# A written-out schedule replaced: two row tiles and both filter pieces at the head of the loads, and a new order of all steps

## Chip, cores and metric

The kernel runs on one core of a Trainium2 chip. The metric is the device time of one execution in microseconds; lower is better. The time before is 196.86 us, the median of three runs (196.56 to 197.38).

## What is computed

Sequence length 2048, width 512, feed-forward width 1792, one batch, bf16.

```python
xn = layernorm(A_q)                       # over the last axis
# s: a short causal convolution, a gate, a long causal convolution
k_shift[t] = sum_j k[t-3+j] * shift_k[:, j]          # 4 taps
kv = k_shift * v
y  = causal_conv(kv, ssm_k) + kv * ssm_D             # 2048 taps for each of 512 channels, by FFT in the reference
s  = xn * y
# g: a gated feed-forward block
g  = silu( (gelu(xn @ w_gate) * (xn @ w_up)) @ w_down )
out = A_q + s * g
```

## The kernel before

The feed-forward half works on four quarters of the sequence, q = 0 to 3, each of four row tiles of 128 rows. For each quarter and each of 14 column groups m of w_gate and w_up (Wg, Wu), TensorE makes two products of four matmuls (steps psg and psu), ScalarE takes gelu of the first (GE), and VectorE multiplies it with the second (HT). Four matmul groups with w_down (Wd) for each row tile follow (psd). The first two column groups of quarter 0 are done in halves of 256 columns, so that they can begin when only row tiles 0 and 1 are there. Their input xnT is the normalised x (XN), transposed by TensorE (psxn) and copied out of PSUM by ScalarE or VectorE.

The long convolution is a two-stage Fourier transform done with matmuls. The filter arrives as four pieces of 512 KB, Hn0 to Hn3. Hn0 and Hn1 are transposed by TensorE (psh), copied out (HTr), and multiplied with the transform table F (steps ps1H, copies AH); the result is written to DRAM (ZH, eight writes of 256 KB issued on ScalarE's queue). Hn2 and Hn3 are permuted by four ScalarE copies into HP, transposed by DMA into HTD, and go through ps1J, copies AJ and eight more writes to ZH on SP's queue. AJ has four buffers, so the fifth copy needs the first write to have landed. The signal kv is made by VectorE from KK, V and four tap rows SKB (copied by GpSimd from SKR): 32 long instructions, each quarter ending in KV0 to KV3. It goes through ps1K and AK to ZK. Second stages (psf for the filter, psk for the signal, psi for the way back) use 32-row matmuls; BH, BK, HS, HW, BO and ZI are their buffers, MI and G1 their tables, which three DMA transpositions on SP's queue make. The last matmuls (psy) bring y back into sequence order, and VectorE joins both halves. Weights come in four pieces, of 2, 4, 4 and 4 column groups.

Nothing on the chip decides an order. The program makes 788 tasks with numbers; the string `SEQ` lists these numbers, and every engine's instructions are emitted in the order of that list. A trailing `b` gives a task to the second engine that it allows (VectorE instead of ScalarE). Loads and most writes are issued on SP's queue in the order of the list too, so each queue runs in order and a step that waits holds up all behind it on its engine. The string `ORDER` numbers the loads: `x01` is row tile 0 of x alone, `x22` tiles 2 and 3, `h` a filter piece, `w` a pair of w_gate and w_up pieces, `s` the taps, `d` half of w_down. The class `Sched` computes planned times for the tasks in the list's order; on the chip this matters only in one way: when a step takes a buffer or PSUM bank from a pool, it is given the one that is planned to be free first.

```python
t.start, t.eng = max(base, free.get(eng, 800.0)), eng
...
f, b.slot = b.pool.find()
```

Eleven matmuls on zeros (`warm_up`) precede the first real step.

Of the kernel before, what the change touches and what calls it, by code (L numbers as in the profile page):

```python
# [16 lines left out]
NT = 16  # L17
# [5 lines left out]
LAST = [(0, 384), (384, 512)]  # L23
TURN = 8192
N_WARM = 11
ORDER = "x01 h0 x11 h1 x22 w0 w1 h2 h3 D0 w2 s0 k0 v0 x1 w3 k1 v1 d0 d1 k2 v2 k3 v3 x2 x3"
SEQ = (
# [22 lines left out]
)  # L50
NF_BANKS = 4
ISSUE = 470.0
LOAD_NS = {("x0_", 262144): 1400.0, ("x0_", 131072): 450.0, 262144: 900.0, 524288: 1350.0, ("x", 524288): 2100.0, ("h", 524288): 1300.0, ("wg", 524288): 1550.0, ("wu", 524288): 1450.0, 917504: 2620.0, ("sk", 524288): 1500.0, 344064: 1250.0, 46080: 350.0, 3072: 100.0, 1024: 200.0}
W_XT, W_SW, W_BK, W_BH, W_ZI, W_BI, W_ZK, W_MI, W_G1 = 1665000, 600000, 555000, 703000, 333000, 640000, 490000, 740000, 222000
NC_PAIRS = 4
SMALL = 1.15 * 262144
# [235 lines left out]
class Sched:  # L292
# [2 lines left out]
    SEM = 90.0  # L295
    DMA_LAT = 2000.0
    LOAD_LAT = 2450.0
    HEDGE = 600.0
    DMA_BW = 370.0
    SHARE_BW = 300.0  # L300
    FIRST = {"loads": 1050.0, "SP": 30500.0}
    DRAIN = 121.0
    EARLY, TAKEN, SHARED, WAIT = (0.0, 1.0), 1400.0, 46000.0, 3300.0
    LANDS = (3150.0, 3490.0, 5770.0)

    def __init__(self):
        self.tasks = []
# [35 lines left out]
                t.deps.append(d)  # L343

    def run(self):
        free = dict(self.FIRST)
        pipe = 0.0
        n_loads = 0
        order = []
        pmode = 0  # L350
        for name in SEQ.split():
            t = self.tasks[int(name.rstrip("b"))]
            eng, dur = t.opts[name[-1] == "b"]
            base = 0.0
            for d in t.deps:
                base = max(base, d.end if eng == d.eng == "PE" else d.end + d.lat + (self.SEM if not d.nbytes or eng != "PE" else 400.0 if d.eng == "loads" else self.HEDGE))
            for b in t.w:
                if b.pool is not None and b.slot is None:
                    f, b.slot = b.pool.find()
                    b.pool.take(b.slot)  # L360
                    base = max(base, f + self.SEM)
            t.start, t.eng = max(base, free.get(eng, 800.0)), eng
            free[eng] = t.end = t.start + dur + (self.DRAIN if eng == "PE" and t.mode != pmode else 0.0)
            pmode = t.mode if eng == "PE" else pmode
            if eng == "loads":
                free[eng] = t.start + dur * (self.EARLY[1] if t.start < self.EARLY[0] else 1.0)
                if n_loads < len(self.LANDS):
                    free[eng] = self.LANDS[n_loads] - self.LOAD_LAT
                n_loads += 1
                t.end = free[eng] + self.LOAD_LAT  # L370
            elif t.nbytes:
                en = t.end
                if en < self.SHARED:
                    free["loads"] += self.TAKEN
                pipe = max(pipe, en + self.DMA_LAT / 2) + t.nbytes / (self.SHARE_BW if en < self.SHARED else self.DMA_BW)
                t.end = pipe + self.DMA_LAT / 2 + (self.WAIT if en < self.SHARED else 0.0)
            for b in set(t.r + t.w):
                b.left -= 1
                b.last_end = max(b.last_end, t.end + t.lat)
                if b.left == 0 and b.pool is not None:  # L380
                    b.pool.release(b.slot, b.last_end)
            order.append(t)
        assert sorted(t.n for t in order) == list(range(len(self.tasks)))
        return order
# [6 lines left out]
def act(n, sb=False):  # L391
    return 170.0 + n * 0.833 + (30.0 if sb else 0.0)


def dve(n, rate):
    return 150.0 + n / 0.96 / rate


def build_kernel(nc, A_q, A_k, A_v, A_shift_k, A_ssm_k, A_ssm_D, B_w_gate, B_w_up, B_w_down, out):
    with ExitStack() as es0:  # L400
# [56 lines left out]
        Hn = at("Hn", [128, KD, S_LEN], BF16, g_at)  # L457
        HTr = at("HTr", [128, NT // 2, DM], BF16, kk_at - 16384)
        HP = at("HP", [128, NT, 2, 128], BF16, kk_at - 8192)
# [139 lines left out]
        def op(engs, fn, r=(), w=(), rr=(), ww=(), lat=0.0, after=()):  # L599

            def emit(e):
                R = rr() if callable(rr) else rr
                W = ww() if callable(ww) else ww
                trk.op(e, lambda h: fn(e, h), r=R, w=W)
            return S.add(engs, emit, r=r, w=w, lat=lat, after=after)
# [284 lines left out]
        h_perm, h_dtr = [], []  # L890
        d_htd = [dsem(f"d_htd{hf}") for hf in range(2)]
        for hf in range(2):
            for k in range(2):
                h_perm.append(op([("ACT", act(1024, True)), ("DVE", dve(1024, 1))], lambda e, h, hf=hf, k=k: copy(e, h, HP[:, 8 * hf:8 * hf + 8, k, :], Hn[:, 2 + k, :].rearrange("p (a t) -> p t a", t=NT)[:, 8 * hf:8 * hf + 8, :]),
                                 r=[bHn[2 + k]], w=[bHP[hf]], rr=[R_Hn[2 + k]], ww=[R_HP[hf]]))
        for hf in range(2):
            def dtr(e, hf=hf):
# [294 lines left out]
        for j in range(8):  # L1192
            p = B(f"psy{j}", pC)
# [93 lines left out]
```

## Time and profile before

| | |
|---|---|
| median of three runs | 196.86 us |
| profiled execution | 195.77 us |
| its span, first to last instruction | 194.0 us |
| TensorE busy | 187.5 us (97%) |
| VectorE busy | 159.8 us (82%) |
| ScalarE busy | 125.5 us (65%) |
| DMA | 49.19 MB, mean 254 GB/s |
| granted TensorE clock | 1.000 |

A row of the timeline gives the start in us, the time from the first start to the last end of the merged instructions, the engine, the line, the operation, output and input tiles, the shape and the count; in brackets stands the idle time of the engine ahead of it and what ended it. `SPq` and `ACTq` rows are DMA issues on a queue. A matmul row's length contains the modelled end of the last matmul, so the distance between starts is the better measure of pace. Line 618 is the helper through which all plain matmuls go, line 609 the helper for ScalarE's copies, line 590 the helper for DMAs.

### The profile page before, as it was taken

The numbers are of one execution on the slowest core, as the hardware profiler recorded it, in microseconds if no ns is written. First come the engines' busy times: TensorE is split into PE (matmuls) and PEld (weight loads), VectorE is DVE, ScalarE is ACT, GpSimd is POOL, SyncE is SP. The second block draws the span as 40 slices with busy tenths as digits, with TensorE's granted clock in tenths as the row PEclk, the third lists the DMA queues.
The fourth block names the chain that finished last, engine by engine and source line by source line (L and its number), as shares of the span: only waits on it lengthen the run. The fifth ranks groups of instructions, "written<-read, shape, count | busy, mean of one in ns | idle before, by whom it ended". The sixth has DMA issues, their size and how long they took to land.

```text
span 194.0 us, 3492 instructions
## 1 busy us (share of the span) xinstructions
PE 187.5 (97%) x1364; PEld 85.0 (44%) x1377; DVE 159.8 (82%) x245; ACT 125.5 (65%) x170; POOL 14.0 (7%) x32
## 2 busy tenths in 40 slices
PE   7799999999998999999999999999999999999993
PEld 2594544444443444443434433433444434444442
DVE  7599699998999993977788789878897963588993
ACT  6787999979876978868648767756577531222121
POOL 6412420000000000020300000000000000000000
PEclk9999999999999999999999999999999999999999
DMA  5999999999999859999999991893714344939333
GB/s 165 327 322 349 377 403 315 188 217 375 368 363 355 242 210 231 384 345 283 277 306 221 318 312 41 291 332 106 237 37 184 105 150 135 402 109 363 126 139 135
DMA packets 46102, 49.19 MB, mean 254 GB/s; under 512 B 12803, under 2 KB 39943, under 8 KB 46086
## 3 DMA queue, kind: packets, MB, share of 16 engines
q1 hardware_dynamic: 37510, 42.67, 69.8%
q10 hardware_dynamic: 8576, 6.29, 10.1%
q8 instruction: 11, 0.18, 0.4%
q14 instruction: 5, 0.04, 0.1%
HBM read 27.39 MB, written 14.68 MB: 217 GB/s over the span
## 4 chain that ended last, share of the span: by engine, by line
PE 87%; DMA 7%; ACT 2%; issue 1%; SPq 1%; DVE 1%
PE psall L618 80%; PE psall L1028 5%; DMA Hn<-in_A_ssm_k_dram 3%; DMA ZH<-X 3%; SPq L590 1%; PE psall L854 1%; ACT G L609 1%; PE psall L878 1%; ACT X L609 1%; ACT ASX L609 0%; ACT GE L1137 0%; DVE G L1175 0%; DVE G L1174 0%; ACT G L1172 0%
## 5 line engine op out<-in xcount | busy, mean ns | idle before, releaser
L618 PE MATMUL psall<-xnT,Wu 128*128 128x512 bf16 (+1 forms) x232 | 55.8, 372 | 0.0
L618 PE MATMUL psall<-xnT,Wg 128*128 128x512 bf16 (+1 forms) x232 | 55.3, 372 | 0.0
L618 PE MATMUL psall<-Wd,HT 128*128 128x512 bf16 (+2 forms) x231 | 50.8, 366 | 0.7 <-issue 0.5
L1140 DVE TENSOR_TENSOR HT<-psall,GE 128x512 bf16<-128x512 f32 x54 | 36.7, 685 | 15.2 <-PE psall L618 13.6
L1137 ACT ACTIVATE GE<-psall 128x512 bf16<-128x512 f32 x54 | 31.7, 601 | 12.6 <-PE psall L618 12.2
L618 PEld LDWEIGHTS psall<-Wd,HT 128*128 128x128 bf16 x238 | 22.4, 98 | 25.9 <-issue 1.1
L618 PEld LDWEIGHTS psall<-xnT,Wu 128*128 128x128 bf16 x232 | 21.6, 98 | 25.9 <-issue 3.8
L618 PEld LDWEIGHTS psall<-xnT,Wg 128*128 128x128 bf16 x232 | 21.9, 98 | 25.3 <-issue 1.3
L609 ACT ACTIVATE X<-psall 128x1024 bf16<-128x1024 f32 (+1 forms) x18 | 15.1, 846 | 3.8 <-DMA ZH<-X 3.3
L609 ACT ACTIVATE HS<-psall 128x1024 bf16<-128x1024 f32 x14 | 13.7, 1022 | 4.2 <-PE psall L1028 4.2
L1164 ACT ACTIVATE G<-psall 128x512 bf16<-128x512 f32 x12 | 7.0, 597 | 12.8 <-PE psall L618 12.4
L1011 DVE TENSOR_TENSOR KAC<-KAC,KTM 128x2048 bf16<-128x2048 bf16 x12 | 14.6, 1218 | 0.1
L1009 DVE TENSOR_TENSOR KTM<-KK,SKB 128x2048 bf16<-128x2048 bf16 x12 | 14.6, 1217 | 0.0
L609 ACT ACTIVATE BO<-psall 128x1024 bf16<-128x1024 f32 x9 | 9.1, 1023 | 8.2 <-PE psall L1028 7.7
L821 DVE BATCH_NORM_STATS2 stats<-X 128x6 f32<-128x512 bf16 x16 | 10.3, 677 | 3.9 <-DMA X<-in_A_q_dram 3.9
L609 ACT ACTIVATE KB<-psall 128x1024 bf16<-128x1024 f32 x11 | 11.0, 1021 | 3.6 <-PE psall L1028 3.6
L609 ACT ACTIVATE AST<-psall 128x1024 bf16<-128x1024 f32 x12 | 12.3, 1031 | 1.2 <-PE psall L618 1.0
L612 DVE CAST BO<-psall 128x1024 bf16<-128x1024 f32 x7 | 8.5, 1223 | 3.7 <-PE psall L1028 3.7
L1172 ACT ACTIVATE G<-psall 128x512 bf16<-128x512 f32 (+2 forms) x5 | 2.6, 512 | 13.1 <-PE psall L618 13.1
L1091 DVE TENSOR_TENSOR HW<-KB,HW 128x1024 bf16<-128x1024 bf16 x16 | 10.9, 682 | 0.0
L1091 DVE TENSOR_TENSOR HS<-KB,HS 128x1024 bf16<-128x1024 bf16 x16 | 10.8, 682 | 0.0
L618 PE MATMUL psall<-V,F 128*128 128x512 bf16 x30 | 8.8, 379 | 0.4 <-ACT ASX L609 0.3
(83 smaller groups left out, 172.2 us busy)
## 6 DMA issues: line engine op xcount, KB each, us to landing
BH<-ZH SPq DMA_DIRECT2D x8, 512.0 KB, 6.3
HW<-HS SPq DMA_DIRECT2D x16, 256.0 KB, 2.9
BK<-ZK SPq DMA_DIRECT2D x8, 512.0 KB, 5.1
ZI<-BO ACTq DMA_DIRECT2D x16, 256.0 KB, 2.9
BI<-ZI SPq DMA_DIRECT2D x8, 512.0 KB, 4.1
ZK<-AST SPq DMA_DIRECT2D x6, 512.0 KB, 3.7
Hn<-in_A_ssm_k_dram SPq DMA_DIRECT2D x4, 512.0 KB, 8.4
KK<-in_A_k_dram SPq DMA_DIRECT2D x4, 512.0 KB, 8.8
```

The costliest lines, as they stand in the source:

```text
L609: return h.activation(o, i, ACTF.Copy, scale=scale)
L612: return h.tensor_copy(o, i)
L618: return h.matmul(o, lhsT=l, rhs=r, start=st, stop=sp)
L821: t_stats[t] = op([("DVE", 670.0)], lambda e, h, t=t: h.bn_stats(stats[:, t, :], X[:, t, :]), r=[bX[q][t % 4]], w=[bst[t]], rr=[R_X[t]], w ...
L1009: op([("DVE", dur)], lambda e, h, j=j, m=m: h.tensor_tensor(KTM[:, m.slot, :, :], kk(j), sk(j), ALU.mult), r=need + [bSKB[j], a], w=[m], r ...
L1011: op([("DVE", dur)], lambda e, h, m=m: h.tensor_tensor(KAC[:, a.slot, :, :], KAC[:, a.slot, :, :], KTM[:, m.slot, :, :], ALU.add), r=[m], ...
L1028: trk.op("PE", lambda h: h.matmul(ps(s, i)[b, :], lhsT=wt(col)[a, :], rhs=data(col)[a, :], start=n < 16, stop=n >= len(todo) - 16, tile_po ...
L1091: return hd.tensor_tensor(o, flat(KB, kb[h]), o, ALU.mult)
L1137: op([("ACT", act(512))], lambda e, h: h.activation(GE[:, g.slot, :], bank(pg), ACTF.Gelu_apprx_tanh), r=[pg], w=[g], rr=lambda: R_bank(pg ...
L1140: op([("DVE", dve(512, 1))], lambda e, h: h.tensor_tensor(HT[:, q % 2, m, :], bank(pu), GE[:, g.slot, :], ALU.mult), r=[pu, g], w=[bHT[q][m]],
L1164: op([("ACT", act(n))], lambda e, h, g=g, pc=pc: h.activation(g, pc(), ACTF.Tanh, scale=0.5), r=[p], w=[bt], rr=lambda p=p: R_bank(p), ww= ...
L1172: op([("ACT", act(n))], lambda e, h, g=g, pc=pc: h.activation(g, pc(), ACTF.Silu), r=[p], w=[bt], rr=lambda p=p: R_bank(p), ww=rg, after=z ...
```

## The change

`ORDER` starts with `x02 h0 h1 x22` instead of `x01 h0 x11 h1 x22`: row tiles 0 and 1 come as one load of 256 KB, and the first two filter pieces precede tiles 2 and 3. There are 787 tasks instead of 788, all numbers from 20 on are lower by one, and the whole of `SEQ` is new. The planner's constants and its model of transfers are replaced: eight noted landing times for the first loads instead of three, an allowance of 900 ns behind a later load, and the transfers of loads and writes in one line. The four HP copies are now allowed on ScalarE alone, at 2090 ns.

In names, the first loads on SP's queue are, before: X0, X1, Hn0, X2+X3, Hn1, Wg0, Wu0, X of quarter 1, Wg1, KK0, D, Wu1, Hn2, KK0, Wg2, SKR, KK0, KK1, Wu2, Wg3, Wu3, Hn3, V3, V0, KK2, HTD0, HTD1. After: X0+X1, Hn0, Hn1, X2+X3, Wg0, Wu0, X of quarter 1, Wg1, KK0, Wu1, D, Hn2, KK0, SKR, Wg2, KK0, KK1, Wu2, Hn3, Wg3, KK4, V0, KK2, Wu3, V3, HTD1, KK3, HTD0.

The first steps of TensorE before: psh0 (two), psxn0_0, psxn0_1, three ps1H halves, psh1 (two), psg0_0 first half. After: psh0 (two), psh1, ps1H5, psh1, ps1H4, ps1H6, ps1H2, psxn0_0, psxn0_1, three ps1H halves, psu0_0 first half, psxn0_2, psxn0_3. The first four writes to ZH stand in ScalarE's list between its first gelus; before, one did.

```diff
-ORDER = "x01 h0 x11 h1 x22 w0 w1 h2 h3 D0 w2 s0 k0 v0 x1 w3 k1 v1 d0 d1 k2 v2 k3 v3 x2 x3"
+ORDER = "x02 h0 h1 x22 w0 w1 h2 h3 D0 w2 s0 k0 v0 x1 w3 k1 v1 d0 d1 k2 v2 k3 v3 x2 x3"
 SEQ = (
-    "17 19 18 0 3 1 2 4 8 5 7 11 21 6 9 51 12 66 67 68 74 20 69 76 75 50 10 77 13 53 22 83 23 84 87 118 70 108 71 72 113 55 73 88 78 79 54 370 52 "
...
+    "0 2 1 3 11 5 4 8 9 12 10 13 7 6 17 18 19 20 50 49 65 53 66 73 67 68 75 74 52b 76 55b 69 51 107 108 54 102 112 96 70 71 77 82 56 72 83 104 "
...
-LOAD_NS = {("x0_", 262144): 1400.0, ("x0_", 131072): 450.0, 262144: 900.0, 524288: 1350.0, ("x", 524288): 2100.0, ...
+LOAD_NS = {("x0_", 262144): 1200.0, ("x0_", 131072): 450.0, 262144: 900.0, 524288: 1430.0, ("x", 524288): 1500.0, ...
-    HEDGE = 600.0
-    DMA_BW = 370.0
-    SHARE_BW = 300.0
-    FIRST = {"loads": 1050.0, "SP": 30500.0}
+    HEDGE, LATE = 1500.0, 900.0
+    DMA_BW = 350.0
+    AHEAD, ISSUE = 6000.0, (480.0, 3000.0)
     DRAIN = 121.0
-    EARLY, TAKEN, SHARED, WAIT = (0.0, 1.0), 1400.0, 46000.0, 3300.0
-    LANDS = (3150.0, 3490.0, 5770.0)
+    LANDS = (4100.0, 5590.0, 6950.0, 8300.0, 9200.0, 10100.0, 11500.0, 12950.0)
...
+            t.eng = eng
             if eng == "loads":
...
+                t.start = max(base, free["SP"])
+                dma = max(dma, t.start + self.LOAD_LAT) + dur
                 if n_loads < len(self.LANDS):
-                    free[eng] = self.LANDS[n_loads] - self.LOAD_LAT
+                    dma = self.LANDS[n_loads]
...
+                if t.nbytes:
+                    t.end = dma = max(dma, t.end + self.DMA_LAT) + t.nbytes / self.DMA_BW
...
-                h_perm.append(op([("ACT", act(1024, True)), ("DVE", dve(1024, 1))], ...
+                h_perm.append(op([("ACT", 2090.0)], ...
```

More of the change, by code (lines that the diff above doesn't have):

```diff
@@ L52 @@
 ISSUE = 470.0
-LOAD_NS = {("x0_", 262144): 1400.0, ("x0_", 131072): 450.0, 262144: 900.0, 524288: 1350.0, ("x", 524288): 2100.0, ("h", 524288): 1300.0, ("wg", 524288): 1550.0, ("wu", 524288): 1450.0, 917504: 2620.0, ("sk", 524288): 1500.0, 344064: 1250.0, 46080: 350.0, 3072: 100.0, 1024: 200.0}
+LOAD_NS = {("x0_", 262144): 1200.0, ("x0_", 131072): 450.0, 262144: 900.0, 524288: 1430.0, ("x", 524288): 1500.0, ("h", 524288): 1400.0, ("wg", 524288): 1700.0, ("wu", 524288): 1550.0, 917504: 2900.0, ("sk", 524288): 1500.0, 344064: 1300.0, 46080: 350.0, 3072: 100.0, 1024: 200.0}
 W_XT, W_SW, W_BK, W_BH, W_ZI, W_BI, W_ZK, W_MI, W_G1 = 1665000, 600000, 555000, 703000, 333000, 640000, 490000, 740000, 222000
@@ L345, in run @@
     def run(self):
-        free = dict(self.FIRST)
-        pipe = 0.0
+        free = {"SP": 700.0}
+        dma = 0.0
         n_loads = 0
@@ L355, in run @@
             for d in t.deps:
-                base = max(base, d.end if eng == d.eng == "PE" else d.end + d.lat + (self.SEM if not d.nbytes or eng != "PE" else 400.0 if d.eng == "loads" else self.HEDGE))
+                base = max(base, d.end if eng == d.eng == "PE" else d.end + d.lat + (self.SEM if not d.nbytes or eng in ("SP", "loads") or d.end < 11000.0 else self.LATE if d.eng == "loads" or eng != "PE" else self.HEDGE))
             for b in t.w:
@@ L361, in run @@
                     base = max(base, f + self.SEM)
-            t.start, t.eng = max(base, free.get(eng, 800.0)), eng
-            free[eng] = t.end = t.start + dur + (self.DRAIN if eng == "PE" and t.mode != pmode else 0.0)
-            pmode = t.mode if eng == "PE" else pmode
+            t.eng = eng
             if eng == "loads":
-                free[eng] = t.start + dur * (self.EARLY[1] if t.start < self.EARLY[0] else 1.0)
+                t.start = max(base, free["SP"])
+                dma = max(dma, t.start + self.LOAD_LAT) + dur
                 if n_loads < len(self.LANDS):
-                    free[eng] = self.LANDS[n_loads] - self.LOAD_LAT
+                    dma = self.LANDS[n_loads]
                 n_loads += 1
[L370 to L376, printed above, removed]
+                t.start = max(t.start, dma - dur - self.LOAD_LAT - self.AHEAD)
+                free["SP"] = t.start + (self.ISSUE[1] if dur > 3000.0 else self.ISSUE[0])
+                t.end = dma
+            else:
+                t.start = max(base, free.get(eng, 800.0))
+                free[eng] = t.end = t.start + dur + (self.DRAIN if eng == "PE" and t.mode != pmode else 0.0)
+                pmode = t.mode if eng == "PE" else pmode
+                if t.nbytes:
+                    t.end = dma = max(dma, t.end + self.DMA_LAT) + t.nbytes / self.DMA_BW
             for b in set(t.r + t.w):
@@ L893, in build_kernel @@
             for k in range(2):
-                h_perm.append(op([("ACT", act(1024, True)), ("DVE", dve(1024, 1))], lambda e, h, hf=hf, k=k: copy(e, h, HP[:, 8 * hf:8 * hf + 8, k, :], Hn[:, 2 + k, :].rearrange("p (a t) -> p t a", t=NT)[:, 8 * hf:8 * hf + 8, :]),
+                h_perm.append(op([("ACT", 2090.0)], lambda e, h, hf=hf, k=k: copy(e, h, HP[:, 8 * hf:8 * hf + 8, k, :], Hn[:, 2 + k, :].rearrange("p (a t) -> p t a", t=NT)[:, 8 * hf:8 * hf + 8, :]),
                                  r=[bHn[2 + k]], w=[bHP[hf]], rr=[R_Hn[2 + k]], ww=[R_HP[hf]]))
```

42 rows, old and new, of the table SEQ are left out of this document.

## The prediction

> **What bounds the kernel now.** I read the page's engine shares and chain first, then busy time of TensorE in four stretches, then the rows around the stretches where it was idle.
>
> ```profile
> PE 187.5 (97%) x1364; PEld 85.0 (44%) x1377; DVE 159.8 (82%) x245; ACT 125.5 (65%) x170; POOL 14.0 (7%) x32
> PE 87%; DMA 7%; ACT 2%; issue 1%; SPq 1%; DVE 1%
> ```
>
> ```profile
> 6.04:10.41 4.37, 3.55 (x30) 1.00 1.04 348
> 10.41:61.00 50.59, 50.38 (x271) 1.00 1.07 328
> 61.00:63.00 2.00, 1.49 (x7) 1.00 1.06 361
> 63.00:190.25 127.25, 126.46 (x1040) 1.00 0.70 225
> ```
>
> Columns of the second fence: stretch, its length, PE busy (matmuls), granted clock, DMA share, GB/s. TensorE is the bound: from 10.41 to 61 it idles 0.21 us, and the clock is 1.00 in every stretch. The change removes no matmul, so only idle time can be won, and any new wait of TensorE is lost whole. There are two places with idle time.
>
> ```profile
> 6.04 1.27 PE L878 MATMUL psall<-ident,Hn 128*128 128x128 f32 x8 [0.19 <-DMA Hn<-in_A_ssm_k_dram]
> 7.14 0.61 PE L854 MATMUL psall<-ident,XN 128*128 128x128 bf16 x8
> 7.98 0.83 PE L618 MATMUL psall<-HTr,F 128*128 128x256 bf16 x6 [0.23 <-ACT HTr L609]
> 9.40 1.17 PE L878 MATMUL psall<-ident,Hn 128*128 128x128 f32 x8 [0.59 <-DMA Hn<-in_A_ssm_k_dram]
> ```
>
> ```profile
> 59.93 1.24 PE L618 MATMUL psall<-Wd,HT 128*128 128x512 bf16 x5
> 61.37 0.60 PE L618 MATMUL psall<-HTD,F 128*128 128x512 bf16 x2 [0.20 <-ACT X L609]
> 62.28 0.61 PE L618 MATMUL psall<-V,F 128*128 128x512 bf16 x2 [0.31 <-ACT ASX L609]
> ```
>
> ```profile
> 60.29 1.02 ACT L609 ACTIVATE X<-psall 128x1024 bf16<-128x1024 f32 x1 [0.99 <-DMA ZH<-X]
> ```
>
> At the start the first filter piece lands just before 6.04 and the second at 9.4. Near 61 ScalarE stood in its order behind a copy into a buffer whose write to ZH had not landed. Four full matmuls follow each other in 0.86 us (the rows at 29.93 and 30.79 below), so 0.216 each: five from 59.93 end at 61.01, the next comes 0.36 late, and two from 61.37 end at 61.80, the next comes 0.48 late. Together 0.84.
>
> The profiled execution took 195.77 (span 194.0); the runs shown have a median of 196.86, lowest 196.56. The profile is 1.09 under the median, so the executions timed lose about that much more, at places this trace cannot show. I add differences from the trace to the median. A difference of 0.5%, 1.0 us, is about what a measurement of this kernel can tell.
>
> **The change part by part.** Planner constants reach the chip only through which free buffer a step is given; the label of the permuting copies (HP, now 2090 ns on ScalarE alone) moves nothing, as all four ran there already. Both lists switch TensorE between full and 32-row mode 48 times. Twenty-four copies swap engine, twelve each way: at most 0.3 us on engines with 18% and 35% idle. What counts is order.
>
> *Start.* Four loads stand ahead of the first weights instead of five: row tiles 0 and 1 (256 KB), Hn0, Hn1, tiles 2 and 3. No byte is saved before the first w_up piece. The old landings follow from who waited for them: Hn0 6.0, tiles 2 and 3 8.0 (the statistics of 7.99 below), Hn1 9.4. Cumulated, 0.75 MB were in by 6.0, 1.0 MB by 8.0, 1.5 MB by 9.4; Hn1 now completes 1.25 MB, which is 8.7 on that line. At the other end, the landings written into the diff have Hn1 at 6950 ns, and the old ones had Hn0 at 5770, 0.27 before the matmuls that it released at 6.04, so 7.2. TensorE's pace after the start is set by ScalarE, through which the normalised tiles 2 and 3 go last.
>
> ```profile
> 6.90 1.02 ACT L609 ACTIVATE HTr<-psall 128x1024 bf16<-128x1024 bf16 x1 [1.36 <-PE psall L878]
> 7.82 1.08 ACT L609 ACTIVATE xnT<-psall 128x512 bf16<-128x512 bf16 x2
> 7.99 0.69 DVE L821 BATCH_NORM_STATS2 stats<-X 128x6 f32<-128x512 bf16 x1 [1.27 <-DMA X<-in_A_q_dram]
> 8.78 1.04 ACT L609 ACTIVATE HTr<-psall 128x1024 bf16<-128x1024 bf16 x1
> 12.14 0.60 ACT L609 ACTIVATE xnT<-psall 128x512 bf16<-128x512 bf16 x1 [0.23 <-PE psall L854]
> ```
>
> A 1024-wide copy takes 0.92 start to start (6.90 to 7.82), a 512-wide one 0.48 (two from 7.82 to 8.78). ScalarE's new order is HTr, AH, HTr, AH2, AH, AH, AH, xnT, xnT: three wide, six narrow, 5.64 us. It starts at 7.35 (the first eight transposes end at 7.31) and ends at 13.1 if nothing is late; if Hn1 decides, the second HTr starts 1.5 after its landing (4 transposes 0.55, two matmuls of 256 columns 0.22, 4 transposes 0.55, and 0.17 of modelled end, 1.03 less 0.86) and the last xnT ends 4.4 after that, so at 5.9 after the landing: 13.1 for 7.2, 14.6 for 8.7. At the old pace TensorE would reach its first matmul on tiles 2 and 3 at 13.69: in the trace that is at 12.82, behind the copy of 12.14, and the new list puts two full and four half matmuls more ahead of it (0.87). DVE's part (tiles 2, 3 at 8.5, statistics, two copies it takes over, normalising) puts that matmul at 13.3 in the fast case. So the start gives 0.4 or costs 0.9. I take a cost of 0.1, an Hn1 near 7.9, between the two.
>
> *Loads from 15 to 34.* In the new list four writes of transformed filter tiles to ZH (ScalarE's queue) are issued right after the start, at about 14 to 17.5; the old list has one at 16.93 and the next at 21.68. SKR now precedes the third w_gate piece; Hn3, KK4, V0 and KK2 precede the last w_up piece.
>
> ```profile
> 4.99 0.51 SPq L590 DMA_DIRECT2D Wg<-in_B_w_gate_dram  x1
> ...
> 12.83 0.44 SPq L590 DMA_DIRECT2D Wu<-in_B_w_up_dram  x1
> ...
> 16.93 0.38 ACTq L590 DMA_DIRECT2D ZH<-X  x1
> ...
> 21.68 0.37 ACTq L590 DMA_DIRECT2D ZH<-X  x1
> ...
> 22.16 3.42 POOL L986 COPY SKB<-SKR 128x512 bf16<-128x512 bf16 x4 [3.86 <-DMA SKR<-in_A_shift_k_dram]
> ...
> 23.17 0.43 SPq L590 DMA_DIRECT2D KK<-in_A_k_dram  x1
> ```
>
> ```profile
> Wg<-in_B_w_gate_dram SPq DMA_DIRECT2D x1, 512.0 KB, 9.6
> ```
>
> ```profile
> Wu<-in_B_w_up_dram SPq DMA_DIRECT2D x1, 512.0 KB, 12.6
> ```
>
> ```profile
> KK<-in_A_k_dram SPq DMA_DIRECT2D x1, 512.0 KB, 11.2
> ```
>
> ```profile
> ZH<-X ACTq DMA_DIRECT2D x1, 256.0 KB, 8.1
> ```
>
> ```profile
> 22.13 1.03 PE L618 MATMUL psall<-xnT,Wg 128*128 128x512 bf16 x4
> 25.59 1.89 PE L618 MATMUL psall<-xnT,Wu 128*128 128x512 bf16 x8
> 29.93 1.03 PE L618 MATMUL psall<-xnT,Wg 128*128 128x512 bf16 x4
> 30.79 1.89 PE L618 MATMUL psall<-xnT,Wu 128*128 128x512 bf16 x8
> ```
>
> The one-line fences give the time to landing of the issues at 4.99, 12.83, 23.17 and 16.93: they landed at 14.6, 25.4, 34.4 and 25.0. Same bytes ahead means the same landing: the new third w_gate piece lands where SKR did, 22.1; the third w_up piece is still at 25.4; the last w_up piece is where KK2 was, 34.4 (six pieces after 25.4, 1.5 each), and the last w_gate piece, two pieces on, at 28.4. The readers, from the matmuls ahead of them in the two lists: w_gate third 22.13 less two full plus two half, 21.9; w_up third 25.59 plus two half less eight row transposes of 0.055 (eight in 0.61 less 0.17), 25.4; w_gate last 29.93 less four full and twelve transposes plus two half, 28.6; w_up last 31.65 (the second four of the row at 30.79) plus eight full and two half, 33.6. All four lie within 0.8 us of their readers, on either side.
>
> To this come two corrections. A faster front shifts all landings by 0 to -1.5 (the noted landing of the second w_gate piece is 12.95, in the trace 14.6); I take -0.3, as the bytes are the same. And three more writes are under way by 25.4. One costs nothing if it fills gaps, and its bytes if not:
>
> ```profile
> 12.00:24.00 12.00, 11.95 (x78) 7.06 (x77) 10.50 (x24) 10.34 (x18) 3.13 (x6) 1.00 1.07 345
> ```
>
> 256 KB at 345 GB/s with the engines at a share of 1.07: 0.76 us, three 0 to 2.3. The write of 16.93 got 256 KB in 8.1 us, so four will not have passed by 25.4; I take 0.9. Then the third w_up piece lands at 26.0 against 25.4 + 0.1: 0.5 lost. The last one lands at 34.4 - 0.3 + 0.4 (one write more by then) = 34.5 against 33.6 + 0.1 + 0.5: 0.2 lost.
>
> The Trainium skill, DMA: Bandwidth & Descriptors, section Queues, rings and completion order, says that each DMA engine alternates between the queues that have work, a packet at a time. The trace agrees in that the write landed while loads were queued, but its 8.1 us is far under an equal part. By an equal part the four writes would pass at once; that is priced as a rival.
>
> *Middle.* The new list has the copies of stage J earlier against their writes and moves the first MI transposition behind them, so that the first reuse of a J buffer waits only for the write that follows V1 on SP. I count the 0.84 at 61 as won; SP's first J write stood there behind this:
>
> ```profile
> 44.16 6.98 SPq L1039 DMA_TRANSPOSE MI<-TFA  x1
> ...
> 54.98 3.38 SPq L1039 DMA_TRANSPOSE MI<-TFB  x1
> ```
>
> What is late next is VectorE's KV0: it ended at 43.67, its reader began at 44.82; the reader now stands twelve full matmuls earlier, at 42.2, and VectorE's list has 1.6 us less ahead of KV0, so 1.15 of slack becomes about 0.2.
>
> ```profile
> 42.45 1.22 DVE L1013 TENSOR_TENSOR V<-KAC,V 128x2048 bf16<-128x2048 bf16 x1
> ...
> 44.82 0.59 PE L618 MATMUL psall<-V,F 128*128 128x512 bf16 x2
> ```
>
> *End.* The last four output blocks keep their order on TensorE; nothing.
>
> Sum: +0.1 + 0.5 + 0.2 - 0.84 = 0.0, so 196.9.
>
> **The rivals.** *Faster:* the noted landings are right. The start gives 0.4, every piece lands 0.8 to 1.5 earlier than I took and no reader waits, the 0.84 goes: -1.24, 195.6, and down to 194.5 if the 1.09 between profile and median also was such waits. For it: the old note for Hn0 held within 0.27. Against: the same bytes stand ahead. It decides if Hn1 is in by 7.3.
>
> *Slower by late weights:* writes take their full bytes and Hn1 lands near 8.7, so that loading the filter first does not do what it says. Then the third w_up piece lands at 25.4 + 2.3 = 27.7 against 25.4, 2.3 lost (a late start is inside this, not beside it), less 0.84: +1.5, 198.4. It decides once the third w_up piece lands after 26.2. For it: DMA share of 1.07; the new notes give the landing of the second w_gate piece as a constant, behind which the four writes are not counted.
>
> *Slower at 61:* the fourth J write stands on SP behind the second MI transposition. If that takes 6.98 instead of 3.38, the write is 3.6 later, and with it the last J copy. Twenty-four full matmuls, 5.2 us, stand in the list between that copy's product and the next one that needs its banks; the copies up to it take some 2.6 of these (two of 0.92, one of 0.6, and the gelu's wait), so 2.6 is covered and 1.0 lost, and the 0.84 is not won: 196.9 + 0.84 + 1.0 = 198.7. Against: the write is also issued earlier than its old counterpart.
>
> **How the numbers follow.** Even, 196.9 (its own range 196.1 to 197.9): 0.33. Faster, 195.6: 0.30. Late weights, 198.4: 0.27. At 61, 198.7: 0.10. The edges of the even case give 0.03 to faster and 0.02 to slower: faster 0.33, same 0.28, slower 0.39. The range runs from 194.8, near the end of the faster case, to 199.2 (196.86 plus the 2.3 of the writes, nothing won back).
>
> **What would show it.** Right: Hn1 in by 8; the first matmul on row tile 2 at 13.3 to 14.2; a TensorE wait of some 0.5 before the matmuls of the third w_up piece near 25.5 and a smaller one near 34; no TensorE gap between 55 and 65. Wrong: Hn1 by 7.3 and gapless TensorE from 13 (faster); TensorE idle over 1.5 between 20 and 35 (late weights); ScalarE waiting on ZH with TensorE behind it near 62 to 66. Any large wait after 80 would be a place that I have not priced.

## The result and the profile after

| | median | ratio to before, 95% interval |
|---|---|---|
| before (beside it) | 196.93 us | |
| changed kernel | 199.71 us | 1.0124 [1.0091, 1.0158] |

Medians count all executions; the ratios, here and below, leave out those more than 1.5% above the fastest of their kernel (here 201.72 and 203.80 us). By the ratio the changed kernel is 1.2% slower, some 2.4 us. The prediction was 196.9, with a range up to 199.2; the median is above it. The first profile is of the execution of 203.80 us; the profile read here is of a second set of runs of the same kernel (label changed_again): 199.13 us, span 197.3, clock 1.000. That is 3.36 more than the 195.77 of the profile before.

The page's engine shares and chain, of the changed kernel:

```profile
PE 189.1 (96%) x1377; PEld 84.6 (43%) x1377; DVE 158.6 (80%) x245; ACT 126.4 (64%) x170; POOL 13.3 (7%) x32
...
PE 75%; DVE 8%; DMA 8%; ACT 3%; issue 3%; ACTq 1%; SPq 1%; DVEq 0%
```

Busy time by stretch, in the prediction's stretches (the last one longer by the longer span); columns: stretch, its length, TensorE busy (matmuls), weight loads, VectorE, ScalarE, GpSimd, clock, DMA share, GB/s:

```profile
6.04:10.41 4.37, 3.87 (x35) 3.04 (x34) 3.61 (x9) 3.62 (x5) 1.39 (x5) 1.00 0.99 299
10.41:61.00 50.59, 46.83 (x248) 22.63 (x247) 44.04 (x64) 38.94 (x56) 5.84 (x9) 1.00 1.03 303
61.00:63.00 2.00, 2.00 (x11) 0.88 (x9) 2.00 (x3) 1.73 (x2) 0.00 (x0) 1.00 1.14 388
63.00:193.50 130.50, 130.50 (x1062) 55.38 (x1061) 103.72 (x152) 77.68 (x103) 2.56 (x4) 1.00 0.73 230
```

Before, TensorE idled 0.21 us from 10.41 to 61 and 0.51 from 61 to 63. Now it idles 3.76 in the long stretch and nothing from 61 to 193.5. The gap near 61 is gone, as forecast, and a larger loss stands ahead of it. The next rows say where. TensorE and ScalarE on the timeline of the changed kernel, at the start, from 21 to 36, and near 53:

```profile
6.85 0.71 PE L877 MATMUL psall<-ident,Hn 128*128 128x128 f32 x4 [0.20 <-DMA Hn<-in_A_ssm_k_dram]
...
11.25 0.60 PE L617 MATMUL psall<-xnT,Wu 128*128 128x256 bf16 x4 [0.56 <-DVE xnT L611]
...
13.53 0.60 PE L617 MATMUL psall<-xnT,Wg 128*128 128x256 bf16 x4
...
21.03 0.60 ACT L608 ACTIVATE X<-psall 128x512 bf16<-128x512 f32 x1 [1.99 <-DMA ZH<-X]
...
25.88 1.04 PE L617 MATMUL psall<-xnT,Wu 128*128 128x512 bf16 x4 [0.26 <-DMA Wu<-in_B_w_up_dram]
...
35.28 1.02 PE L617 MATMUL psall<-xnT,Wu 128*128 128x512 bf16 x4 [0.70 <-DVE KTM L1008]
...
42.88 0.51 ACTq L589 DMA_DIRECT2D ZH<-X  x1
...
52.16 1.94 ACT L608 ACTIVATE X<-psall 128x1024 bf16<-128x1024 f32 x2 [2.71 <-DMA ZH<-X]
...
53.24 0.60 PE L617 MATMUL psall<-V,F 128*128 128x512 bf16 x2 [1.84 <-ACT X L608]
...
54.16 0.61 PE L617 MATMUL psall<-HTD,F 128*128 128x512 bf16 x2 [0.31 <-ACT X L608]
```

The row of 52.16 holds the loss that was not priced. It is the first J copy, AJ4, into X12. ScalarE stood 2.71 us ahead of it, not for data, but because AH1, a copy of the first half, had used the same buffer, and AH1's write to ZH, issued at 42.88, landed at 52.08. TensorE ran out of PSUM banks behind it and lost 1.84 and 0.31 in these rows. Before, AJ4 had the same buffer and did not wait:

```profile
48.97 1.02 ACT L609 ACTIVATE X<-psall 128x1024 bf16<-128x1024 f32 x1
```

There the copy ahead of it in X12 was AH2, whose write had landed at 38.66. The first profile of the changed kernel has the gap of 53.24 too, longer: 3.09 us, as AH1's write landed at 53.52. The row of 35.28 names KTM as releaser, but VectorE's KTM is no input of these matmuls; the last w_up piece landed at 35.14, and that is what they waited for.

Modelled matmul ends hide part of each gap, so the rest goes by a *lag*: the start of a TensorE step in the trace, less the summed lengths of all TensorE steps ahead of it (0.216 us for a full matmul, as in the prediction; the planner's lengths for the others). It rises where TensorE loses time. Some matmul records are missing from the traces; in the last six rows one is missing just at 34, and that entry stands 0.2 too high.

| lag, us | at 13 | at 34 | at 51 | at 64 | end |
|---|---|---|---|---|---|
| before | 2.85 | 2.64 | 2.60 | 3.42 | 9.19 |
| changed_again | 2.69 | 4.31 | 6.77 | 6.74 | 12.56 |
| before_shared_buffer | 2.39 | 2.32 | 4.68 | 4.65 | 10.42 |
| before_nine | 1.70 | 1.79 | 1.74 | 1.72 | 7.48 |
| j_buffers_swapped | 2.42 | 4.34 | 5.11 | 5.08 | 12.04 |
| eight_buffers | 2.52 | 4.41 | 4.52 | 4.49 | 10.40 |
| eight_free_h | 2.55 | 5.17 | 4.91 | 4.88 | 10.87 |
| eight_short_writes | 3.07 | 3.08 | 3.57 | 3.54 | 13.84 |
| eight_late_writes | 2.20 | 2.79 | 4.30 | 4.27 | 11.01 |
| eight_and_k | 3.20 | 4.98 | 4.73 | 4.70 | 10.52 |
| changed_all | 2.42 | 2.77 | 3.08 | 3.05 | 9.39 |

(A step counts to the column by its place in the sum, so the wait at 53 stands under 51.) Changed less before, from one column to the next: start -0.16, loads from 13 to 34 +1.83, 34 to 51 +2.50, the gap at 61 -0.85, after 64 +0.05. The sum is 3.37, against the 3.36 between the two profiled times.

### The profile page after: what moved, and what is told of

It reads as the page before. It is cut to its first block, busy times and chain, and to the rows that moved or that the text cites. A ratio compares the mean times of both kernels' runs of the same rounds, so it can differ in the third digit from the quotient of the medians.

```text
span 202.0 us, 3499 instructions
## 1 busy us (share of the span) xinstructions
PE 189.7 (94%) x1364; PEld 84.6 (42%) x1377; DVE 158.7 (79%) x245; ACT 126.7 (63%) x170; POOL 13.3 (7%) x32
## 4 chain that ended last, share of the span: by engine, by line
PE 64%; DMA 21%; SPq 6%; ACT 3%; issue 2%; DVE 2%; ACTq 0%
PE psall L617 59%; DMA Wu<-in_B_w_up_dram 6%; SPq L589 6%; DMA ZH<-X 5%; PE psall L1027 5%; DMA ZK<-AST 3%; DMA X<-in_A_q_dram 3%; DMA ZI<-BO 3%; ACT AST L608 1%; DVE stats L820 1%; ACT X L608 1%; ACT BO L608 1%; ACT KB L608 0%; DVE xnT L611 0%; ACT GE L1136 0%
## 5 line engine op out<-in xcount | busy, mean ns | idle before, releaser
L617 PE MATMUL psall<-xnT,Wu 128*128 128x512 bf16 (+1 forms) x232 | 57.5, 377 | 0.9 <-DVE xnT L611 0.5
L617 PE MATMUL psall<-Wd,HT 128*128 128x512 bf16 (+2 forms) x230 | 51.4, 366 | 0.7 <-issue 0.5
L617 PEld LDWEIGHTS psall<-xnT,Wg 128*128 128x128 bf16 x232 | 21.9, 98 | 25.9 <-issue 1.7
L608 ACT ACTIVATE HS<-psall 128x1024 bf16<-128x1024 f32 x15 | 15.0, 1025 | 3.7 <-PE psall L1027 3.7
L608 ACT ACTIVATE X<-psall 128x512 bf16<-128x512 f32 (+1 forms) x16 | 12.5, 821 | 6.4 <-DMA ZH<-X 5.5
L608 ACT ACTIVATE BO<-psall 128x1024 bf16<-128x1024 f32 x11 | 11.0, 1023 | 6.5 <-PE psall L1027 5.2
L1165 DVE SCALAR_TENSOR_TENSOR G<-G,psall 128x512 bf16<-128x512 bf16 x12 | 8.0, 681 | 4.3 <-ACT G L1163 4.3
```

Of the source, the lines that this page charges most:

```text
L608: return h.activation(o, i, ACTF.Copy, scale=scale)
L617: return h.matmul(o, lhsT=l, rhs=r, start=st, stop=sp)
L1165: op([("DVE", dve(512, 1))], lambda e, h, g=g, pc=pc: h.scalar_tensor_tensor(out=g, in0=g, scalar=1.0, in1=pc(), op0=ALU.add, op1=ALU.mult ...
```

## The experiments

Theory A: the four early ZH writes make the weights late. Theory B: the first J copy waits for a buffer. Every kernel below fixes all buffers to those of the kernel that it starts from, so that only the named edit differs. Ratios are to the kernel before, run on the same chip beside it (medians 195.6 to 196.6).

**Twice the changed kernel.** changed_again: 1.0133 [1.0101, 1.0165], from two of its four executions; changed_third: 1.0183 [1.0133, 1.0233], above what was expected. The change thus costs 1.2 to 1.8%, by the set of runs.

> The changed kernel once more, for a second profile beside the first. Theory A (weights late): TensorE loses about 1.6 us between 17 and 36 before the matmuls of w_gate and w_up, in every execution, and the rest of the loss is small or varies. Theory B (buffer of the first J copy): most of the loss, and all of its spread, is ScalarE waiting near 44 to 54 for the last write of the first half to ZH, before the copy AJ4. Time 198.6 to 199.9 by both; B has the idle time of TensorE after 45 vary by over 1 us between this profile and the first.

> The changed kernel itself, beside the next three on one chip, for its price without the noise between chips. Both theories: 1.010 to 1.016 times before.

### The buffer of the first J copy

**j_buffers_swapped**

```diff
-AJ4: X12  AJ0: X14  AJ3: G4   AJ1: G6   AJ2: X12  AJ6: X14  AJ5: G4   AJ7: G6
+AJ4: G4   AJ0: G6   AJ3: X12  AJ1: X14  AJ2: G4   AJ6: G6   AJ5: X12  AJ7: X14
```

> Only the buffers of the eight J copies are changed: the first two go to G (free since the filter was transposed) and the next two to X, where the first half's last writes leave from; every order stays. Theory B: the wait before AJ4 goes, 197.6 to 198.4, and the executions lie closer together. Theory A: within 0.3 us of the changed kernel.

Median 198.51, ratio 1.0108 [1.0069, 1.0147]: just above B's range, and only 0.3% under changed_again on the same chip, with intervals that overlap. In the trace B's wait is gone: the lag rises by 0.77 from 34 to 51 in place of 2.46. But the end is only 0.5 lower. Rows of its timeline:

```profile
42.41 1.96 ACTq L589 DMA_DIRECT2D ZH<-X  x1
...
49.42 1.09 PE L617 MATMUL psall<-HTD,F 128*128 128x512 bf16 x4 [0.58 <-ACT AST L608]
...
79.75 2.08 ACT L608 ACTIVATE AST<-psall 128x1024 bf16<-128x1024 f32 x2 [2.10 <-PE psall L617]
```

The wait of 49.42 is for a copy on ScalarE that is late because issuing a ZH write took ScalarE 1.96 us. Further on, the lag rises by 0.68 at 80.8 and by some 0.5 near 133.8, where changed_again had lost nothing. The row of 79.75, ahead of the loss at 80.8, is the same kind of wait once more: a copy of the signal's first stage. It names TensorE as releaser, but the write to ZK from the copy's buffer landed at 79.66. The loss near 133.8 is not explained.

**before_shared_buffer**: theory B put into the kernel before.

```diff
-AH6: X10  AH7: X12  AH2: X12
+AH6: X12  AH7: X10  AH2: X10
```

> The kernel before, with only buffer numbers of three first-half copies exchanged: AH6 in X12, AH7 and AH2 in X10. So the first J copy, AJ4 in X12, follows ZH6, the last write of the half, which landed at 52.1 in the profile of before, where it had followed ZH2, landed at 38.7. Theory B: AJ4 starts near 52.3 in place of 49.0, TensorE gets gaps of 2 to 3 near 52, and the kernel takes 198.5 to 199.8. Rival (the loss near 53 in the changed kernel comes from its order): within 0.7 of before.

Median 198.40, ratio 1.0147 [1.0085, 1.0208], just below the 198.5 that was expected at least. ScalarE and TensorE on its timeline:

```profile
51.86 1.94 ACT L609 ACTIVATE X<-psall 128x1024 bf16<-128x1024 f32 x2 [3.10 <-DMA ZH<-X]
...
52.94 0.60 PE L618 MATMUL psall<-HTD,F 128*128 128x512 bf16 x2 [2.23 <-ACT X L609]
```

Three buffer numbers, with no instruction moved, put the same two rows into the old kernel. This is the strongest evidence for B. The 1.5% is not the wait alone, though: four of the six executions had a granted clock of 0.990 or 0.991 and took 198.39 to 198.65 us, while the two at 0.998 and 1.000 took 196.99 and 197.31, 1.4 and 1.7 above the 195.60 of before beside it. That fits the trace: 2.4 us of lag near 53, less the 0.8 near 61 that is no longer lost. (On the lower clock see the last section.)

**eight_buffers** and **before_eight_buffers**: four more J buffers, in the part of G that nothing uses between the HP copies and BH.

```diff
-"J": [... for T, j in ((X, 12), (X, 14), (G, 4), (G, 6))]
+"J": [... for T, j in ((X, 12), (X, 14), (G, 4), (G, 6), (G, 8), (G, 10), (G, 12), (G, 14))]
```

The J copies take them in their order: G4, G6, G8, G10, G12, G14, X14, X12.

> The changed kernel, its J copies given eight buffers in place of four (G8, G10, G12 and G14 are idle then), so that no J copy shares a buffer with a copy of the first half whose write is still under way, nor with an earlier J copy; lists and all else as in the changed kernel. Theory B (the first J copy waits for a buffer): ScalarE waits for no ZH write, TensorE's gaps of 2.0 and 0.5 near 53 are gone; 197.6 to 198.5, at or a little below the kernel with the buffers swapped (198.5). Rival (the copies are late because the data or ScalarE's issue of the writes is late, whatever the buffer): above 199.0.

> The kernel before with eight J buffers and nothing else changed. The waits of ScalarE for J writes near 58, 60 and 63 go, and with them TensorE's gap of 0.84 near 61: theory B says 0.8 below before, 195.8 to 196.2. Rival (the copies near 61 are then late by something else, or the gap is won and lost again behind): within 0.4 of before.

In the changed list: 197.73, ratio 1.0101 [1.0069, 1.0133], within what was expected; the lag rises by 0.3 from 34 to 51 (the 0.2 taken off), in place of 2.46. In the old list: 194.74, ratio 0.9944 [0.9911, 0.9978], 0.9 us under the 195.60 of before beside it, as B had it: the gap near 61 too came from a buffer whose write was under way.

### The K copies near 80

**eight_and_k** and **before_nine**: the copies AK6 (and AK7 in the changed list) get a buffer without a write under way.

```diff
-"K": [AST[:, j, :, :, :] for j in range(2)] + [ASX[:]]
+"K": [AST[:, j, :, :, :] for j in range(2)] + [ASX[:], G[:, 4:8, :].rearrange("p (i c) d -> p i c d", c=2)]
```

> As eight_buffers, and two copies of the signal's first stage moved to other buffers: AK6 into G4 to G7 (idle then) in place of AST0, where ZK2 landed at 80.5 in the changed kernel and AK6 stood behind it; AK7 into AST0 in place of AST1 (ZK5, 83.1). Theory K (what the freed J buffers won is taken back near 80, where the K copies wait for writes of ZK): TensorE's gaps near 80 to 83 go; 0.4 to 1.0 below eight_buffers, ratio to before 1.003 to 1.007, and so 0.6 to 1.2 per cent below the changed kernel of this call. Rival (nothing is taken back; the J copies were worth 0.3 per cent): 1.008 to 1.011.

> The kernel before with eight J buffers (as before_eight_buffers) and AK6 in G4 to G7 in place of AST0, where it started at 78.6, right behind the landing of ZK2. Theory K: a further 0.3 to 0.7 below before_eight_buffers, ratio 0.990 to 0.993. Rival: 0.994 to 0.996, as with the J buffers alone.

eight_and_k: 197.40, ratio 1.0054 [1.0028, 1.0080], as theory K had it, and 1.3% under changed_third beside it (1.0183). So buffers alone, J's and K's, are worth most of the change's loss. How much of it is J's and how much K's stays open: eight_buffers ran beside other runs of before, the intervals meet, and its own profile loses nothing near 80. before_nine: 194.63, ratio 0.9901 [0.9862, 0.9939], the fastest of all and 1.0% below the kernel before. Its interval meets that of before_eight_buffers (194.74 on another chip), so what the K buffer adds there is not shown by the times. The copy AK6 before, in before_eight_buffers and in before_nine, and the busy time of before_nine:

```profile
78.59 3.05 ACT L609 ACTIVATE AST<-psall 128x1024 bf16<-128x1024 f32 x3 [0.17 <-DMA ZK<-AST]
```

```profile
78.64 3.05 ACT L609 ACTIVATE AST<-psall 128x1024 bf16<-128x1024 f32 x3 [0.72 <-DMA ZK<-AST]
```

```profile
76.61 2.13 ACT L609 ACTIVATE G<-psall 128x1024 bf16<-128x1024 f32 x2
```

```profile
36.00:52.00 16.00, 15.95 (x75) 7.28 (x75) 14.96 (x18) 14.09 (x21) 0.00 (x0) 1.00 1.07 310
52.00:64.00 12.00, 11.95 (x56) 5.41 (x56) 12.00 (x14) 9.47 (x13) 0.00 (x0) 1.00 1.12 339
```

From 52 to 64 TensorE idles 0.05 us. The copy of 78.59 waited only 0.17, yet it had no room: with the J waits gone it waited 0.72, and TensorE lost 0.5 us behind it. In G it does not wait.

### The late weights

**last_wup_early**: the last w_up piece ahead of KK4, V0 and KK2 on SP's queue.

```diff
-g3 KK4 V0 KK2 u3 V3
+g3 u3 KK4 V0 KK2 V3
```

> Only the load of the last w_up piece is moved, from behind KK4, V0 and KK2 to ahead of them. Theory A: it lands about 4.3 us earlier, the wait before its first matmul (about 0.5 us of the 1.6) goes, 0.4 to 0.6 us faster than the changed kernel. Theory B: no change beyond 0.2, as the time lost later swallows it.

Three executions took 199.5 to 200.2 and one 196.1, so there is no ratio. The trace shows the piece in time: no wait near 35, the lag at 34 is 3.70 in place of 4.31. J's wait behind it stayed (1.56 and 0.48 near 53), and the time with it.

**writes_spread**: three of the four early writes 6 to 13 us later.

```diff
-... ZH2 ... ZH6 ZH4 ... ZH5 ...
+... ZH2 ... (gelu 2) ZH6 ... (gelu 9) ZH4 ... (gelu 6) ZH5
```

> Only three of the four early writes to ZH are moved in ScalarE's list: from 15 to 16 us to about 22, 26 and 28, nearly where the kernel before had its second to fourth. Theory A with the writes as its cause: the third w_gate, third w_up and last w_gate pieces land 0.5 to 2 us earlier, TensorE loses at most 0.7 instead of 1.6 by 36, and the time falls by 0.7 to 1.0. If instead the new order of loads alone makes the pieces late: under 0.3 us. Theory B: no change beyond 0.3.

199.71, ratio 1.0151 [1.0122, 1.0180]; theory A expected a gain and there was none. The writes, issued at 22.7, 25.8 and 27.9, landed at 31.9, 34.9 and 36.6. Two of the three were still through before the last w_up piece, at 34.9 in place of 35.1. The move was too short to tell anything.

**eight_short_writes**: eight_buffers, with the four early writes cut to 16 partitions.

```diff
-dma(e, dst, al, ...)
+dma(e, dst[0:w], al[0:w], ...)      # w = 16 for AH2, AH6, AH4, AH5; rows 16 to 127 are written by four transfers behind J writes
```

> As eight_buffers, but the four early ZH writes of the first half carry 16 of their 128 partitions; the other 112 are written from J buffers by four further transfers near 53 to 60 (the values of these rows are then not those of the reference). Theory A (the four early writes, 1 MB, hold up the weights): the third w_gate and w_up pieces land near 21 and 24 in place of 22 and 26, the last w_up piece near 33 in place of 35, and TensorE's waits between 17 and 36 fall from 1.7 to under 0.5; 196.4 to 197.3, 1.0 to 1.5 below eight_buffers. Rival (the order of the loads, with Hn3, KK4, V0 and KK2 ahead of the last w_up piece and SKR ahead of the third w_gate piece, makes them late): waits fall by under 0.5, time within 0.5 of eight_buffers.

199.53, ratio 1.0169 [1.0082, 1.0257], far above what was expected, and yet A's point holds. The stretch from 17 to 36, of eight_buffers and then of this kernel:

```profile
17.00:36.00 19.00, 17.46 (x92) 7.98 (x92) 16.16 (x21) 15.67 (x20) 3.91 (x5) 1.00 1.10 361
```

```profile
17.00:36.00 19.00, 18.95 (x102) 9.20 (x102) 17.59 (x25) 16.70 (x21) 4.31 (x5) 1.00 1.10 334
```

TensorE idles 0.05 us there, not 1.54, and the lag does not rise from 13 to 34. (It stood 0.55 higher at 13, and a later start gives the weights more time; at 34 it is 1.3 lower.) The third and last w_up pieces landed at 24.8 and 33.4, not at 25.6 and 35.0. What was won was lost again near 77, as a row of ScalarE's timeline shows:

```profile
76.74 1.02 ACT L608 ACTIVATE ASX<-psall 128x1024 bf16<-128x1024 f32 x1 [3.61 <-DMA ZK<-ASX]
```

A K copy stood 3.61 us behind a ZK write, after the four added transfers on the same queue. This cost comes from the experiment, so its total time says nothing on A.

**eight_free_h**: AH7 into G0 in place of X10, where it waited for ZH2 near 21 (1.99 in the row above, 2.6 in eight_buffers).

```diff
-AH7: X10
+AH7: G0
```

> As eight_buffers, and the copy AH7 into G0, which is idle, in place of X10, where ZH2 (issued at 12.3, landed at 21.7) held ScalarE for 2.6 before 21.69. Theory S (of the loss between 17 and 36 the larger part is ScalarE standing behind that write, so that gelus, VectorE's products and PSUM banks come late): ScalarE's wait on ZH near 21 and TensorE's 1.27 near 27.8 go; 0.7 to 1.3 below eight_buffers, a ratio to before of 1.004 to 1.007. Theory A (the weights themselves land late): TensorE then waits for the third w_up piece instead, landing near 25.6, and the time is within 0.4 of eight_buffers, ratio 1.008 to 1.011.

198.05, ratio 1.0113 [1.0076, 1.0151]: no gain, theory S falls. ScalarE no longer waits, and TensorE waits for the third w_gate piece (lag +1.37 at 23.0) and the last w_up piece (+0.77 at 35.9) instead.

**eight_late_writes**: a buffer of its own for each first-half copy, and the four writes behind the weights.

```diff
-... ZH2 ... ZH6 ZH4 ... ZH5 ... (gelu 12) ZH3
+... (gelu 12) ZH2 ZH6 ZH4 ZH5 ZH3
```

> As eight_free_h, with a buffer of its own for each first-half copy, and the four early ZH writes issued near 33.5, behind the last weights, in place of 12 to 16. No byte is left out. Theory A (the bytes of these writes delay the weights): third w_gate piece lands near 21.2, third w_up near 24.5, last w_up near 33.5; TensorE loses under 0.4 between 17 and 36; another 0.5 to 1.0 below eight_free_h unless the writes, moved, delay kv's loads behind: ratio 0.998 to 1.004. Theory S alone: within 0.4 of eight_free_h.

197.19, ratio 1.0049 [1.0016, 1.0083]: theory A's direction, its size just missed. From 17 to 34 only the third w_gate piece is still waited for (0.59 at 21.9). Then comes a new wait:

```profile
38.78 0.60 ACT L608 ACTIVATE xnT<-psall 128x512 bf16<-128x512 bf16 x1 [2.71 <-issue]
```

```profile
39.43 1.04 PE L617 MATMUL psall<-xnT,Wg 128*128 128x512 bf16 x4 [1.42 <-ACT xnT L608]
```

ScalarE issued five writes in a row from 33.74, the last two taking 1.52 and 1.86 us. The copy behind them was late.

**eight_load_order** and **eight_both**: eight_buffers, and eight_free_h, with two loads moved.

```diff
-... SKR g2 ... g3 KK4 V0 KK2 u3 V3
+... g2 SKR ... g3 u3 KK4 V0 KK2 V3
```

> As eight_buffers, with two loads moved on SP's queue: the third w_gate piece ahead of SKR, and the last w_up piece ahead of KK4, V0 and KK2, as in the kernel before. Theory A: the third w_gate piece lands near 20.6 in place of 22.1, the last w_up piece near 31 in place of 35; the waits of 0.55 near 22 and of 0.35 to 0.8 near 35 go; 0.4 to 0.9 below eight_buffers, ratio 1.005 to 1.008, unless the taps, 1.5 later, hold up kv. Theory S: the wait near 27.8 stays, and it takes up again what is won at 22; within 0.4 of eight_buffers.

> eight_free_h and eight_load_order together. If ScalarE's wait and the weights are two separate losses, both go: TensorE's loss between 17 and 36 falls from 1.9 to under 0.4, and the time to within 0.5 of before, ratio 0.999 to 1.003. If the writes' bytes alone count, 1.004 or more.

1.0043 [1.0006, 1.0081] and 1.0058 [1.0027, 1.0090]. The first counts only six of ten executions; the median of all ten, 197.77, is 1.008 times that of before. In its profile (199.07 us) the third w_gate and last w_up pieces landed at 20.74 and 30.76, as theory A said, but TensorE lost more than in eight_buffers, at other places. The better comparison is eight_both against eight_free_h (1.0113) on the same chip: 0.5%, with intervals that just meet, about as much as the place of the writes is worth in eight_late_writes. eight_both missed what I expected: the lag still rises by 1.0 from 13 to 34 (0.60 at the third w_up piece), and 1.29 goes at 80.5, with the K copies.

**changed_all**: eight J buffers, the K buffer, a buffer for each first-half copy, the four writes apart behind the weights, and the load order of eight_load_order.

> The changed kernel with all of it at once: J, K and first-half copies in idle buffers, the four early ZH writes moved behind the weights (one each near 28, 31, 33 and 36, not four in a row), the third w_gate piece ahead of SKR and the last w_up piece ahead of KK4, V0 and KK2. If waits for buffers and late weights are the whole of the loss: TensorE loses under 0.5 between 13 and 75, and the kernel takes 0.996 to 1.001 of before. If the order costs in other ways: 1.003 or more.

195.68, ratio 0.9974 [0.9949, 0.9999]. Busy time of its TensorE in two stretches:

```profile
17.00:36.00 19.00, 18.59 (x100) 8.96 (x100) 17.09 (x23) 16.62 (x21) 2.86 (x5) 1.00 1.11 326
...
52.00:64.00 12.00, 11.95 (x56) 5.48 (x56) 11.96 (x13) 10.91 (x14) 0.00 (x0) 1.00 1.10 358
```

The lag rises by 0.6 from 13 to 64, a little more than was expected; in changed_again it rose by 4.05. changed_third, eight_and_k and changed_all ran on one chip, and no two of their intervals overlap: 1.3% goes with the J and K buffers, another 0.8% with the first-half buffers, the writes and the two loads. With all of it put right, the new list is level with the old kernel or a shade faster. It remains behind the old list with the J and K buffers (194.63).

## Why the prediction was wrong

- **Start, +0.1: close, but for another reason.** The first matmul on row tiles 2 and 3 came at 13.53 (13.3 to 14.2 was said), the lag at 13 is 0.16 lower. But Hn1 was in by 6.85, not at 7.9. The *faster* rival named Hn1 by 7.3 as the point that decides, and that point was met without its gain. Tiles 2 and 3 came only at 8.73. VectorE, which has their statistics ahead in its list, copied the transposed tiles 0 and 1 only at 10.38, and TensorE waited for that (0.56 at 11.25). So VectorE set the pace; the working had ScalarE do so, and VectorE only if all else was early.
- **Loads from 15 to 34, +0.5 and +0.2: right in place, too small.** The waits stood at 25.88 and 35.28, as named. The lag rose by 1.83 against before: 0.42 and 0.83 at these two places, 0.37 in smaller steps, and 0.21 by which it fell in before. The term that was mis-sized is the writes' share at the last w_up piece. It was taken to land at 34.5 and came at 35.14, because all four writes had passed by then (the last landed at 30.58) and a part of their bytes had been taken. The third w_up piece was right (26.0 taken, 25.83 found). The third w_gate piece, moved behind SKR, was called level with its reader; it was nearly so here, but cost 0.39 and 1.30 us of idle time in eight_buffers and writes_spread. The rival *late weights* did not happen by its own condition (the third w_up piece after 26.2), though its 2.3 was nearer than my 0.7.
- **Middle, -0.84: the step that failed.** The gap at 61 did go (-0.85), and the 2.50 near 53 came. The working counted "the first reuse of a J buffer" as the only wait, that is, a J copy behind another J copy. But the J pool shares X12 and X14 with the first half's copies, so its first use of them is a reuse too. In both lists AJ4 is given X12. In the old one the copy ahead of it there is AH2, in the new one AH1, whose write is the last of the half. Whether the new order or the new constants put AH1 there, no run separates. The wait cost 2.50 where the sum had nothing. Matching each J copy with the write ahead of it would have shown a bound in the trace of before: its last first-half write landed at 52.14, and AJ4 started at 48.97. KV0, which the prediction named as late next, kept 0.57 of slack (0.2 was said).
- **The rival at 61** had the right kind of wait (ScalarE behind a ZH write, TensorE behind its banks), but at another write, 8 us later.
- **After 64, nothing: right** (+0.05). The K copies near 80 became a limit only in experiments that won time ahead of them.
- **Sum:** -0.16 + 1.83 + 2.50 - 0.85 = +3.3 in the profiled execution. Without the 2.50 it would have been 0.8, inside the range, but only because the late weights (1.83 against 0.7) and the gap at 61 partly cancel.

## What to carry to other kernels

When a schedule changes, list for every pool which step now follows which in each buffer, and when the transfer out of that buffer lands; exchanging three buffer numbers cost the old kernel 1.4 and 1.7 us at full clock, and 2.8 to 3.1 at a clock of 0.99. A copy that waits for a write holds its whole engine's list, so look for the last write of one stage under the first copies of the next, and for memory that is idle just then. Time won ahead of such a copy comes back as its wait, so look for the next one in line before counting a gain: j_buffers_swapped took away 1.7 us of TensorE's loss near 53, and 0.5 us was left of it at the end.

## What the runs showed of the hardware

- A small write between loads is slow by its bytes, not only by its place. With some ten loads queued, the four early 256 KB writes of changed_again took 8.6, 10.0, 12.6 and 14.8 us to land, one behind the other every 2.9 to 3.8 us, some 70 to 90 GB/s of the 363 moved from 17 to 36. The same writes cut to 32 KB took 5.3 to 5.9 us. The group of all eight writes on ScalarE's queue, changed and before:

```profile
ZH<-X ACTq DMA_DIRECT2D x8, 256.0 KB, 9.1
```

```profile
ZH<-X ACTq DMA_DIRECT2D x8, 256.0 KB, 7.5
```

- The Trainium skill (DMA: Bandwidth & Descriptors, section Queues, rings and completion order) has each DMA engine take the queues in turn, a packet at a time. The writes' fifth to quarter of the bytes agrees with it only if the packets of the writes, whose rows are 512 bytes long, are the smaller ones; no run here varied the row.
- Issuing a write can take ScalarE much longer than the usual 0.37 us: 1.87 for the fourth early write (changed_again), 1.52 and 1.86 for the last of five in a row (eight_late_writes), 1.96 near 42 (j_buffers_swapped). ScalarE started nothing else in that time. One to four earlier writes were under way; the issues near 42 in changed_again, with as many, took 0.40 to 0.51, so what decides it is not shown.
- A gap of TensorE was followed by a lower clock in two profiles, and so cost twice. In the first profile of the changed kernel TensorE idled 3.09 us ahead of 54.91, the place of the row of 53.24; from 55.1 on its granted clock was 0.50 for 3.4 us, which is 1.7 us of work (an estimate: half of 3.4). In writes_spread it was 0.50 for 3.4 us from 53.4 on, near the end (53.56) of a gap of 2.14 us. Gaps of 1.84, 1.91 and 2.23 us in this place (changed_again, changed_third, before_shared_buffer) left it at 1.00, so the runs show no length that decides. But of the 30 executions of the six kernels with the J wait, nine had a mean clock of 0.990 to 0.992; of the 91 of the nine other kernels whose profiles have no gap over 1.21 us, none was under 0.997. (eight_late_writes and eight_short_writes, with gaps of 1.42 and 1.65 elsewhere, had three of 13.) The clock row of the first profile's page, in tenths, in 40 slices of 5 us:

```profile
PEclk9999999999979999999999999999999999999999
```
